# Another hand-written order for the first batch of a fused attention and MLP kernel, with four copies moved between engines

## The chip, the cores and the metric

The kernel runs on one core of a Trainium2 chip. The core has five engines with instruction queues of their own, each worked off strictly in order: TensorE (PE, matrix products and transposes), VectorE (DVE), ScalarE (ACT), GpSimd (POOL) and SyncE (SP, which only issues transfers here). They wait for each other through semaphores. The metric is the device time of one execution in microseconds, the median of several runs.

## The reference

Eight batches of 448 tokens, 12 heads of 64. Queries and keys are normalised per head, attention follows, and its output goes, as 768 channels per token, through a layer norm and a two-layer MLP with a residual:

```
q_n, k_n = rmsnorm(q, g_q), rmsnorm(k, g_k)
attn     = softmax(q_n @ k_n^T / sqrt(64))
x        = (attn @ v) as [batch, 448, 768]
xn       = layernorm(x) * g_ln
out      = x + relu(xn @ w_ch1) @ w_ch2        # 768 -> 3072 -> 768
```

All inputs and the output are float32; the kernel multiplies in float16 with float32 sums.

## The kernel before

**Stages.** Attention of batch 0 runs first and alone. From then on attention of batch b+1 is woven between the matrix products of the MLP of batch b; a planner (`attention`, `run_rest`) does that by costs. Only the first stage is ordered by hand: `ORDER` (L39) is a list of words, which `first_attention` (L502) reads from left to right, recording one piece of work for each. Each engine's queue is the subsequence of these pieces that it takes part in. So moving a word moves an instruction in its engine's queue only, and past the others only as far as semaphores say.

**Tiles.** Two heads make a pair; batch 0 has pairs 0 to 5. Pairs come in units: unit 0 is pair 0, unit 1 is pair 1, unit 2 is pairs 2 and 3, unit 3 pairs 4 and 5; units 4 to 6 belong to batch 1 and are prepared towards the end of the stage. A pair's 448 x 2 tokens lie as seven groups of 128 rows, so a unit has 448 elements per partition for each pair (7 groups of 64).

**Words that prepare a unit u** (`pieces`, L237):
- `a`, `c`: squares of keys and queries (L261 on POOL for what `POOL_SQUARE` lists, L263 on ACT otherwise)
- `d`, `e`: their sums (L269, DVE); `gq`, `gk`, `g`: reciprocal root, two ACT steps (L272, L273)
- `i`: keys times the gain product (L283; on DVE for units in `DVE_KG`, on POOL otherwise); for unit 0 it also makes the gain product, through PE
- `j`: the keys' float16 high part (L289 on POOL for `POOL_HI`, L291 on ACT otherwise); `k`: the low part, a subtraction (L294; POOL for `POOL_LO`, DVE otherwise)
- `l`: scaled queries (L86, DVE); `m`: a second copy of them next to the first, so that one transpose fills both halves of the partitions (L334 on ACT for `ACT_DUP`, L336 on POOL for `POOL_DUP`, on DVE otherwise; nothing for units in `TWICE`)
- `z`: values to float16 (L341, L347, POOL)

**Words that work on a pair p:**
- `Kp`: seven transposes of the keys (high and low part side by side, L377 and L380) into one bank `tr`, copied to `kU` (L383 on ACT for `ACT_K`, L385 on DVE otherwise)
- `Qp`: seven transposes of the queries (L397; in a unit of `TWICE` each group is transposed twice, into the upper and the lower 64 partitions), copied to `qU` (L400 on ACT for `ACT_Q`, L402 on DVE otherwise)
- `Sp.i`: scores of group i (L417; for i = 6 two products, L427 and L428) and their exponential on ACT (L433), called Ep.i below. Two score banks alternate, so a score waits for the exponential two before it; nine tiles E alternate, so an exponential also waits for an older `V`.
- `Vp.i`: probabilities times values (L470, L472); after i = 6 DVE divides by the sums (L485 to L492) and so frees the banks for the pair after next
- `Hn`, `Jn`: n filler products of PE whose results nobody reads (L544, L547)

**Other words.** `T` statistics of finished pairs (L653), `A` their aggregate (L668), `Nt` and `Xt` layer norm (L674) and transposes (L710, copied on ACT for t = 0 and 1, on DVE at L718 for t = 2), `R` its root, `Ut` the first up-projections, six products for each of three columns of blocks (L956); `W` loads of MLP weights, `G`, `G2` the layer norm's gain (load and scaling), `L` loads of a unit, `M` some minima. What follows the list begins with the up-projections at L730.

The pieces that the change moves to another engine are these lines:

```
DVE_KG, POOL_HI, POOL_DUP, ACT_Q = (0, 6), (1, 2, 3, 4, 5, 6, *range(8, 25)), (3, 4, 5, 6), (0, 2, 4, 5)
ACT_K, ACT_DUP = (), ()
TWICE = ()
POOL_SQUARE, POOL_LO = ((2, 1), (4, 0), (6, 0), (7, 0), (7, 1)), (5, 6)
```

Of the kernel before, what the change touches and what calls it, by code (L numbers as in the profile page):

```python
# [24 lines left out]
PAIR_UNIT = [(u, w) for u, (_, _, m) in enumerate(UNITS) for w in range(m)]  # L25
UNIT_PAIR = [PAIR_UNIT.index((u, 0)) for u in range(len(UNITS))]
EXP_BIAS = -4.0
DVE_KG, POOL_HI, POOL_DUP, ACT_Q = (0, 6), (1, 2, 3, 4, 5, 6, *range(8, 25)), (3, 4, 5, 6), (0, 2, 4, 5)
ACT_K, ACT_DUP = (), ()
END_WORK = 44  # L30
TWICE = ()
POOL_SQUARE, POOL_LO = ((2, 1), (4, 0), (6, 0), (7, 0), (7, 1)), (5, 6)

# [1 line left out]


ORDER = """  # L39
b0 H12 a0 L4 c0 i0 e0 j0 H24 b1 gq0 d0 k0 l0 a1 m0 K0 G gk0 i1 H10 L5 c1 Q0 d1 j1 H8 S0.0 b2  # L40
S0.1 H5 a2 e1 g1 S0.2 c2 S0.3 k1 l1 z0 d2 e2 m1 K1 S0.4 i2 H16 S0.5 S0.6 H12 Q1 g2 H5 J8 b3 l2
j2 k2 c3 V0.0 S1.0 z2 S1.1 S1.2 V1.0 J8 a3 m2 H4 V0.1 z3 S1.3 K2 S1.4 V0.2 Q2 V0.3 V0.4 d3 S1.5
V0.5 V0.6 S2.0 S1.6 V1.1 V1.2 S2.1 e3 W0 i3 K3 V2.0 S2.2 V2.1 S2.3 Q3 j3 T0 S2.4 k3 V1.3 g3 V1.4
S2.5 S2.6 l3 b4 V1.5 m3 c4 S3.0 S3.1 V2.2 S3.2 K4 a4 V1.6 S3.3 V2.3 S3.4 Q4 d4 V2.4 V2.5 V3.0
V3.1 V3.2 V2.6 i4 S3.5 j4 J4 S3.6 V3.3 T1 K5 e4 k4 S4.0 W1 S4.1 S4.2 Q5 z4 b5 S4.3 V3.4 V4.0
V3.5 S4.4 V4.1 V4.2 S4.5 W2 V4.3 S5.0 g4 V3.6 S4.6 S5.1 J4 V5.0 V4.4 G2 S5.2 l4 T3 K6 V4.5 V5.1
V4.6 S5.3 T4 V5.2 a5 L6 V5.3 S5.4 m4 Q6 i5 S5.5 V5.4 S5.6 V5.5 V5.6 T5 S6.0 S6.1 J4 S6.2 A V6.0
S6.3 V6.1 N0 N1 S6.4 S6.5 J4 V6.2 X0 V6.3 d5 j5 N2 S6.6 V6.4 X1 z5 Q7 c5 V6.5 R U0 e5 U1 g5 X2
V6.6 M k5 U2 K7 b6 L7 a6 L8k c6 i6 l5 m5 e6
""".split()  # L50
DMA_UNIT = 7
PE_SET = (DMA_UNIT + 1) % 2
# [42 lines left out]
class _Fast:  # L95
# [141 lines left out]
    def pieces(self, u):  # L237
# [91 lines left out]
        def qdup():  # L329
            if u in TWICE:  # L330
                return
            out, x = c["qn"][:, :, 1], c["qn"][:, :, 0]
            if u in ACT_DUP:
                nc.scalar.copy(out=out, in_=x)  # L334
            else:
                (nc.gpsimd if u in POOL_DUP else nc.vector).tensor_copy(out=out, in_=x)  # L336
# [50 lines left out]
    def trans_q(self, p):  # L387
# [6 lines left out]
        for i in (6, *range(6)):  # L394
            o, g = ps[:, :, 384:S] if i == 6 else ps[:, i // 3, ts(i % 3, 128)], self.group(p, i)
            for r in (slice(0, D), slice(D, 2 * D)) if u in TWICE else (slice(0, 2 * D),):
                nc.tensor.matmul(o[r], qn[:, g, 0] if u in TWICE else qn[:, g], sh.id16,  # L397
                                 is_transpose=True, start=(i == 6), stop=(i == 5))
# [866 lines left out]
```

## Time and profile before

| | |
|---|---|
| median of 3 runs | 578.69 us (578.44 to 578.82) |
| the profiled execution | 578.23 us, its span 576.7 us |
| PE busy | 563.6 us, 98% of the span |
| DVE busy | 385.5 us, 67% |
| ACT busy | 363.4 us, 63% |
| POOL busy | 210.0 us, 36% |

The span runs from the first to the last instruction on the chip; some 1.5 us of the time lie outside it. The trace lists every instruction with start, duration, engine, line of the code and tile. In a row of the timeline the columns are start, duration (us), engine, line, operation, output and inputs with their shapes, how many alike were merged, and in brackets the idle time before it with what ended it. An engine's next instruction can start somewhat before the end shown of the one before, since ends overlap in a pipeline. A table of windows gives, for each stretch of the span, each engine's busy time and number of instructions.

### The profile page before, as it was taken

To read this page: it belongs to the slowest core of one execution; us is meant where nothing else is said; L and a number is where in the kernel's file an instruction comes from. 1 tells how busy PE (TensorE), PEld (TensorE's weight loads), DVE (VectorE), ACT (ScalarE), POOL (GpSimd) and SP (SyncE) were. 2 spreads that over 40 slices of the span, in tenths; PEclk is the share of its full clock that TensorE was granted. 3 is DMA by queue.
4 is the path that set the end of the run, shared out by engine and by line. 5 is a ranking of instruction groups with operands and counts; after the bars stand their busy time and mean duration, and the time that the engine had idled before them with its cause. 6 is when DMAs were issued, how large, how long until landed. Compare 5 with 4: busy or idle time off the path is not lost.

```text
span 576.7 us, 13800 instructions
## 1 busy us (share of the span) xinstructions
PE 563.6 (98%) x5510; PEld 416.5 (72%) x5510; DVE 385.5 (67%) x832; ACT 363.4 (63%) x672; POOL 210.0 (36%) x226
## 2 busy tenths in 40 slices
PE   6888999999999999999999999999999999999999
PEld 5656666687686867777677768777777777878686
DVE  6989578799757586846667586854756743664424
ACT  5998886457674779457675588647777477323130
POOL 4885855404540721554341521654242410020000
PEclk9999999999999999999999999999999999999999
DMA  8999999968573877968563787958753390030302
GB/s 215 272 237 221 212 200 165 170 180 111 124 134 84 145 151 141 127 140 116 124 91 66 183 139 143 117 139 141 129 62 65 120 112 2 1 109 1 84 2 59
DMA packets 175321, 72.59 MB, mean 126 GB/s; under 512 B 138292, under 2 KB 170212, under 8 KB 175252
## 3 DMA queue, kind: packets, MB, share of 16 engines
q1 hardware_dynamic: 134304, 52.75, 43.9%
q0 software_dynamic: 40352, 18.50, 24.1%
q8 instruction: 44, 0.72, 0.5%
q10 hardware_dynamic: 596, 0.41, 0.3%
q14 instruction: 25, 0.20, 0.1%
HBM read 52.76 MB, written 11.01 MB: 111 GB/s over the span
## 4 chain that ended last, share of the span: by engine, by line
PE 92%; DVE 3%; ACT 3%; issue 1%; DMA 0%; ACTq 0%; DVEq 0%
PE psH L809 34%; PE psP L832 30%; PE psS L417 8%; PE oA L470 5%; PE psC L740 4%; PE psH L730 4%; ACT E L433 2%; PE oB L472 2%; PE psS L423 2%; DVE ssq L269 1%; PE psW L544 1%; PE tr L380 1%; ACT qU L400 0%; PE psW L1003 0%; DMA w<-in_g_k_dram 0%
## 5 line engine op out<-in xcount | busy, mean ns | idle before, releaser
L433 ACT ACTIVATE E<-psS,rr_all 128x448 f16<-128x448 f32 x336 | 204.1, 633 | 49.1 <-PE psS L417 40.4
L809 PE MATMUL psH<-xnT,w 128*128 128x256 f16 (+1 forms) x2016 | 225.7, 261 | 0.0
L809 PEld LDWEIGHTS <-w 128*128 128x128 f16 x2016 | 172.8, 98 | 24.4 <-issue 5.0
L812 ACT ACTIVATE hS<-psH 128x512 f16<-128x512 f32 x150 | 89.7, 598 | 98.0 <-PE psH L809 93.3
L832 PEld LDWEIGHTS <-hS 128*128 128x128 f16 x1080 | 100.0, 98 | 57.4 <-issue 1.1
L832 PE MATMUL psP<-w,hS 128*128 128x384 f16 x672 | 127.0, 326 | 0.0
L417 PE MATMUL psS<-qU,kU 128*128 128x448 f16 x288 | 101.0, 352 | 4.4 <-ACT E L433 2.9
L470 PEld LDWEIGHTS <-E 128*128 128x128 f16 x1008 | 70.3, 98 | 35.6 <-issue 2.6
L283 POOL TENSOR_TENSOR k<-k,gprod 128x896 f32<-128x896 f32 x18 | 39.2, 2180 | 139.8 <-ACT khl L263 86.1
L815 DVE TENSOR_TENSOR hS<-hS 128x512 f16<-128x512 f16 (+1 forms) x119 | 58.3, 496 | 19.3 <-ACT hS L812 17.8
L832 PE MATMUL psP<-w2s,hS 128*128 128x384 f16 (+1 forms) x408 | 69.9, 322 | 0.0
L470 PE MATMUL oA<-v,E 128*128 128x65 f16 x864 | 66.8, 194 | 1.1 <-ACT E L433 0.6
L768 DVE SCALAR_TENSOR_TENSOR x<-psP,rs_all,x 128x384 f32<-128x384 f32 x60 | 36.4, 616 | 41.1 <-PE psP L832 40.5
L472 PE MATMUL oB<-v,E 128*128 128x65 f16 x288 | 52.0, 193 | 0.1
L843 POOL TENSOR_TENSOR x<-x,hS 128x384 f32<-128x384 f32 x21 | 23.4, 1126 | 75.3 <-ACT hS L911 74.6
L485 DVE RECIPROCAL rec_all<-oA 128x6 f32<-128x6 f32 x48 | 9.2, 192 | 53.0 <-PE oA L470 52.9
L220 POOL DMA_DIRECT2D v<-in_v_dram x54 | 41.5, 781 | 4.4 <-PE oB L472 3.3
L417 PEld LDWEIGHTS <-kU 128*128 128x128 f16 x288 | 28.1, 98 | 10.7 <-issue 2.0
L911 ACT ACTIVATE hS<-hS,rs_all 128x384 f32<-128x384 f32 x27 | 14.6, 604 | 33.0 <-DVE hS L815 33.0
L472 PEld LDWEIGHTS <-E 128*128 128x128 f16 x336 | 32.4, 97 | 0.3 <-DVE xl L492 0.2
L86 DVE SCALAR_TENSOR_TENSOR qn<-q,rr_all 128x256 f16<-128x256 f32 (+2 forms) x69 | 25.0, 424 | 6.8 <-ACT rr_all L273 6.7
L269 DVE TENSOR_REDUCE ssq<-khl 128x14 f32<-128x896 f32 (+1 forms) x24 | 25.5, 1061 | 3.7 <-ACT khl L263 3.6
(145 smaller groups left out, 630.5 us busy)
## 6 DMA issues: line engine op xcount, KB each, us to landing
k<-in_k_dram SPq DMA_DIRECT2D x19, 384.0 KB, 4.3
q<-in_q_dram SPq DMA_DIRECT2D x18, 384.0 KB, 4.1
out_dram<-x SPq DMA_DIRECT2D x14, 384.0 KB, 3.0
w<-in_moe_w_ch_dram POOLq DMA_DIRECT2D x3, 1536.0 KB, 14.5
w<-in_moe_w_ch_dram POOLq DMA_DIRECT2D x4, 1152.0 KB, 14.1
v<-in_v_dram POOLq DMA_DIRECT2D x54, 64.0 KB, 4.4
out_dram<-x POOLq DMA_DIRECT2D x9, 384.0 KB, 2.7
qU<-qn SPq DMA_TRANSPOSE x90, 2.9
```

Source lines behind the costliest of these rows:

```text
L220: nc.gpsimd.dma_start(out[:, :, j, 0:D], main[:, :, j])
L269: nc.vector.tensor_reduce(out=c["ssq"][:, n], in_=c["sq", n], axis=AX.X, op=ALU.add)
L283: (nc.vector if u in DVE_KG else nc.gpsimd).tensor_tensor(out=c["t"][1], in0=c["t"][1], in1=sh.gprod.unsqueeze(1).broadcast_to([128, g, D] ...
L417: nc.tensor.matmul(ps[0][:, 0:S], c["main"][:, ts(i, 128)], c["q"][:, ts(h, S)], start=True, stop=True)
L433: nc.scalar.activation(out=o, in_=x[:, 0:S], func=AFT.Exp, scale=self.units[u][3][:, g:g + 1], bias=EXP_BIAS)
L470: nc.tensor.matmul(oA[:, t, cs], E[:, ts(t, 128)], rhs, start=(i == 0 and t == 0), stop=(i == 6 and t == 2))
L472: nc.tensor.matmul(oB[:, cs], E[:, 320:448], rhs, start=(i == 0), stop=(i == 6))
L768: self.nc.vector.scalar_tensor_tensor(out=x, in0=ps, scalar=self.rs[:, b, t:t + 1], in1=x, op0=ALU.mult, op1=ALU.add)
L809: nc.tensor.matmul(ps[:, i], sh.w1[:, dc, ts(f + i, 128)], self.xnT[:, dc, 256 - N:256], start=(i == 0 and dc == 0), stop=(i == k - 1 and ...
L812: nc.scalar.activation(out=hT[:, f:f + k], in_=ps, func=AFT.Relu)
L815: nc.vector.tensor_tensor(out=out, in0=a, in1=c, op=op)
L832: nc.tensor.matmul(bank[x][:, c], a[:, f], w[:, f, c], start=(start and f == 0), stop=(stop and f == HALF - 1))
```

## The change

It gives some pieces of the first stage another engine:

- unit 1's queries are not doubled (`m1` does nothing) but transposed twice on PE (`TWICE`): fourteen transposes of 64 columns instead of seven of 128
- pair 1's keys are copied out of `tr` by ACT instead of DVE
- the queries of pairs 0, 2 and 5 are copied by DVE instead of ACT (pair 4's stay on ACT)
- unit 0's doubling goes from DVE to ACT
- unit 1's high part goes from POOL to ACT
- unit 2's product with the gains goes from POOL to DVE
- unit 4's low part goes from DVE to POOL, unit 6's from POOL to DVE; unit 6's square of queries from POOL to ACT

And it writes the order anew. Of the words moved, these meet the longest queues: unit 0's `c` and `j` go ahead of the 24 fillers, ten fillers go from before `Q0` to behind it, `a1` goes behind `m0`, the sum `d3` goes ahead of the copies of `K2` and `Q2`, the first weight load `W0` behind `j3` on POOL, `l4` ahead of `T3` and `K6`, the scaling of the layer norm's gain (`G2`) behind `m4`, `X2` ahead of `U1`, `K7` and `l5` ahead of `U2`. Fillers are 121 instead of 128. The order of the loads on SP stays as it was.

```diff
-DVE_KG, POOL_HI, POOL_DUP, ACT_Q = (0, 6), (1, 2, 3, 4, 5, 6, *range(8, 25)), (3, 4, 5, 6), (0, 2, 4, 5)
-ACT_K, ACT_DUP = (), ()
+DVE_KG, POOL_HI, POOL_DUP, ACT_Q = (0, 2, 6), (2, 3, 4, 5, 6, *range(8, 25)), (3, 4, 5, 6), (4,)
+ACT_K, ACT_DUP = (1,), (0, 1)
 END_WORK = 44
-TWICE = ()
-POOL_SQUARE, POOL_LO = ((2, 1), (4, 0), (6, 0), (7, 0), (7, 1)), (5, 6)
+TWICE = (1,)
+POOL_SQUARE, POOL_LO = ((2, 1), (4, 0), (7, 0), (7, 1)), (4, 5)
 
 ORDER = """
-b0 H12 a0 L4 c0 i0 e0 j0 H24 b1 gq0 d0 k0 l0 a1 m0 K0 G gk0 i1 H10 L5 c1 Q0 d1 j1 H8 S0.0 b2
-S0.1 H5 a2 e1 g1 S0.2 c2 S0.3 k1 l1 z0 d2 e2 m1 K1 S0.4 i2 H16 S0.5 S0.6 H12 Q1 g2 H5 J8 b3 l2
-j2 k2 c3 V0.0 S1.0 z2 S1.1 S1.2 V1.0 J8 a3 m2 H4 V0.1 z3 S1.3 K2 S1.4 V0.2 Q2 V0.3 V0.4 d3 S1.5
-V0.5 V0.6 S2.0 S1.6 V1.1 V1.2 S2.1 e3 W0 i3 K3 V2.0 S2.2 V2.1 S2.3 Q3 j3 T0 S2.4 k3 V1.3 g3 V1.4
-S2.5 S2.6 l3 b4 V1.5 m3 c4 S3.0 S3.1 V2.2 S3.2 K4 a4 V1.6 S3.3 V2.3 S3.4 Q4 d4 V2.4 V2.5 V3.0
-V3.1 V3.2 V2.6 i4 S3.5 j4 J4 S3.6 V3.3 T1 K5 e4 k4 S4.0 W1 S4.1 S4.2 Q5 z4 b5 S4.3 V3.4 V4.0
-V3.5 S4.4 V4.1 V4.2 S4.5 W2 V4.3 S5.0 g4 V3.6 S4.6 S5.1 J4 V5.0 V4.4 G2 S5.2 l4 T3 K6 V4.5 V5.1
-V4.6 S5.3 T4 V5.2 a5 L6 V5.3 S5.4 m4 Q6 i5 S5.5 V5.4 S5.6 V5.5 V5.6 T5 S6.0 S6.1 J4 S6.2 A V6.0
-S6.3 V6.1 N0 N1 S6.4 S6.5 J4 V6.2 X0 V6.3 d5 j5 N2 S6.6 V6.4 X1 z5 Q7 c5 V6.5 R U0 e5 U1 g5 X2
-V6.6 M k5 U2 K7 b6 L7 a6 L8k c6 i6 l5 m5 e6
+b0 a0 b1 L4 H18 i0 c0 j0 H24 e0 k0 gq0 l0 G d0 m0 a1 gk0 K0 Q0 H10 c1 d1 L5 S0.0 i1 e1 g1 j1 S0.1
+b2 l1 H14 c2 k1 S0.2 a2 H4 d2 e2 i2 m1 z0 j2 S0.3 K1 S0.4 S0.5 Q1 H8 g2 b3 S0.6 c3 J11 S1.0
+S1.1 H20 V0.0 k2 a3 l2 z2 H3 V0.1 m2 S1.2 S1.3 H7 d3 K2 i3 z3 Q2 V0.2 S1.4 V0.3 e3 V0.4 V1.0
+V1.1 V0.5 S1.5 j3 V1.2 V0.6 S2.0 T0 S2.1 S1.6 W0 K3 S2.2 k3 V1.3 S2.3 S2.4 g3 Q3 V2.0 V2.1 S2.5
+S2.6 V2.2 l3 V1.4 S3.0 b4 V1.5 S3.1 V1.6 m3 S3.2 K4 V2.3 a4 S3.3 c4 V3.0 S3.4 V3.1 i4 V2.4 Q4 d4
+V2.5 S3.5 e4 V2.6 S3.6 j4 K5 S4.0 Q5 W1 S4.1 S4.2 b5 V4.0 S4.3 V3.2 k4 z4 V3.3 V3.4 S4.4 V3.5 T1
+V4.1 V4.2 W2 S5.0 g4 V3.6 S4.5 l4 S4.6 S5.1 J1 S5.2 m4 V4.3 V5.0 S5.3 T3 K6 S5.4 V4.4 V5.1 V5.2
+V4.5 V4.6 L6 a5 T4 S5.5 V5.3 V5.4 Q6 S5.6 G2 V5.5 V5.6 T5 S6.0 A S6.1 V6.0 S6.2 S6.3 V6.1 J1
+S6.4 N0 V6.2 N1 S6.5 i5 d5 j5 V6.3 X0 S6.6 V6.4 N2 X1 z5 V6.5 Q7 c5 e5 g5 U0 X2 U1 R V6.6 K7 l5
+U2 M k5 m5 L7 L8k b6 a6 i6 c6 e6
```

## The prediction

> **What bounds the kernel now.** PE is busy nearly throughout, so I read first the busy time by stage (each column an engine).
>
> ```profile
> core 0: us, PE busy (x) PEld busy (x) DVE busy (x) ACT busy (x) POOL busy (x), PEclk, DMA share, GB/s
> 0.00:12.53 12.53, 7.74 (x71) 7.03 (x72) 7.63 (x21) 5.84 (x12) 4.92 (x12) 1.00 0.83 204
> 12.53:56.44 43.91, 36.81 (x497) 26.72 (x497) 40.94 (x80) 39.24 (x76) 32.74 (x32) 1.00 1.10 245
> 56.44:576.70 520.26, 519.02 (x4947) 382.74 (x4944) 336.90 (x734) 318.30 (x586) 172.36 (x184) 1.00 0.65 114
> ```
> From 56.44 us on (first up-projection matmul of batch 0 outside U) PE is idle for 520.26 - 519.02 = 1.2 us in all. The change leaves that part's PE work alone, so it is worth what it moves the moment at which that part begins. Before it lie two stages: up to the first score at 12.53, and 43.9 us in which DVE is busy 93% and ACT 89%.
>
> The timelines of ACT and DVE there say which of the two waits for which.
>
> ```profile
> 11.57 0.91 ACT L400 COPY qU<-psQ 128x896 f16<-128x896 f16 x1 [1.81 <-PE psQ L397]
> 12.91 1.16 ACT L433 ACTIVATE E<-psS,rr_all 128x448 f16<-128x448 f32 x2 [0.44 <-PE psS L417]
> 23.72 0.92 ACT L400 COPY qU<-psQ 128x896 f16<-128x896 f16 x1
> 24.51 1.20 ACT L433 ACTIVATE E<-psS,rr_all 128x448 f16<-128x448 f32 x2
> 29.03 2.76 ACT L433 ACTIVATE E<-psS,rr_all 128x448 f16<-128x448 f32 x5
> 37.29 0.90 ACT L400 COPY qU<-psQ 128x896 f16<-128x896 f16 x1
> 42.70 0.63 ACT L433 ACTIVATE E<-psS,rr_all 128x448 f16<-128x448 f32 x1 [0.41 <-PE psS L417]
> 44.07 2.02 ACT L433 ACTIVATE E<-psS,rr_all 128x448 f16<-128x448 f32 x3
> ```
> E0.0 starts at 12.91. An exponential takes 0.63 and the next follows after (2.76 - 0.63)/4 = 0.53. E2.0, the second of the pair at 24.51, starts at 24.51 + 1.20 - 0.63 = 25.08. E5.6, the last of the three at 44.07, starts at 44.07 + 2.02 - 0.63 = 45.46. From 24.51 on only one gap of ACT (0.41) shows: there ACT sets the pace. A query copy (Q2's at 23.72, Q5's at 37.29) holds it 24.51 - 23.72 = 0.79.
>
> ```profile
> 9.52 1.11 DVE L336 COPY qn<-qn 128x448 f16<-128x448 f16 x1
> 10.55 0.64 DVE L385 COPY kU<-tr 128x960 f16<-128x960 f16 x1
> 12.44 2.08 DVE L294 TENSOR_TENSOR khl<-w2s,khl 128x448 f16<-128x448 f32 x1 [0.20 <-POOL khl L289]
> 16.61 1.07 DVE L269 TENSOR_REDUCE ssq<-qn 128x14 f32<-128x896 f32 x1
> 19.16 0.62 DVE L402 COPY qU<-psQ 128x896 f16<-128x896 f16 x1
> 22.08 0.48 DVE L336 COPY qn<-qn 128x896 f16<-128x896 f16 x1
> 38.59 1.08 DVE L294 TENSOR_TENSOR khl<-k,khl 128x896 f16<-128x896 f32 x1
> 48.48 0.49 DVE L668 BATCH_NORM_AGGREGATE stat<-stat 128x2 f32<-128x24 f32 x3
> 54.43 0.56 DVE L718 COPY w2s<-tr 128x768 f16<-128x768 f16 x1
> 57.76 1.79 DVE L283 TENSOR_TENSOR k<-k,gprod 128x896 f32<-128x896 f32 x1
> ```
> ```profile
> 8.93 1.55 POOL L283 TENSOR_TENSOR w2s<-w2s,gprod 128x448 f32<-128x448 f32 x1 [4.92 <-ACT khl L263]
> 12.37 1.68 POOL L261 TENSOR_TENSOR khl<-w2s 128x896 f32<-128x896 f32 x1
> 16.28 2.08 POOL L283 TENSOR_TENSOR w2s<-w2s,gprod 128x896 f32<-128x896 f32 x1
> 18.42 0.93 POOL L289 CAST khl<-w2s 128x896 f16<-128x896 f32 x1
> 19.29 0.83 POOL L341 CAST v<-w 128x768 f16<-128x768 f32 x1
> 55.07 1.89 POOL L294 TENSOR_TENSOR khl<-hS,khl 128x896 f16<-128x896 f32 x1
> 56.92 1.68 POOL L261 TENSOR_TENSOR qn<-q 128x896 f32<-128x896 f32 x1
> ```
> These two belong together. The copy at 9.52 takes 1.11 for half the elements of the one at 22.08 (0.48), and ends 0.15 after POOL's product (8.93 + 1.55). The subtraction at 12.44 takes 2.08 for half the elements of the one at 38.59 (1.08), beside POOL's square (to 14.05). So DVE's two-operand operations and SBUF copies stand still until POOL's running one ends; reductions and copies out of PSUM do not. The Trainium skill, "SBUF — State Buffer", section "Who interferes with whom", calls it an exclusive lock on a shared port pair, where the second to issue blocks fully; the 0.15 us agrees. By it, the key product that the change gives to DVE costs 1.08 or 1.79 by POOL's work beside it.
>
> **The change part by part.** I follow each engine's queue in the new order, with these durations; 0.05 us stands for a signal between engines, an estimate from PE's 12.53 behind the copy's end at 12.48.
>
> ```profile
> 6.32 2.74 PE L544 MATMUL psW<-id 128*128 128x128 f16 x24
> 9.09 0.85 PE L380 MATMUL tr<-id,khl 128*128 128x128 f16 x6
> 10.80 0.74 PE L397 MATMUL psQ<-id,qn 128*128 128x128 f16 x7
> 12.53 0.54 PE L417 MATMUL psS<-qU,kU 128*128 128x448 f16 x2 [0.55 <-ACT qU L400]
> 17.26 0.83 PE L544 MATMUL psW<-id 128*128 128x128 f16 x12
> 19.85 0.55 PE L417 MATMUL psS<-qU,kU 128*128 128x448 f16 x2
> 55.04 1.17 PE L956 MATMUL psU<-w2s,w 128*128 128x128 f16 x18 [0.42 <-DVE w2s L718]
> ```
> *Start.* Unit 0's duplication (L334, 448 elements) goes to ACT: 0.58, as ACT's squares of that size (row below); bounds 0.58 and the 0.91 of the 896-element copy; I take 0.58. The query scaling, which now ends where the copy at 9.52 starts, has one sum less ahead of it and ends at about 9.2; ACT's duplication then at 9.8. K0 still ends at 9.94 (9.09 + 0.85). Q0 follows at once, without ten fillers between, at PE's slow rate of the start (2.74/24 = 0.11 each): to 10.75. DVE, no longer in the blocked copy, takes it in 0.62: 11.4. S0.0 starts at 11.45 and E0.0 at 11.83 (12.91 - 12.53 = 0.38 later), 1.08 before now.
>
> ```profile
> 9.18 0.58 ACT L263 ACTIVATE qn<-w2s 128x448 f32<-128x448 f32 x1
> 13.96 0.22 ACT L272 ACTIVATE rt<-ssq 128x14 f32<-128x14 f32 x1
> 14.21 0.22 ACT L273 ACTIVATE rr_all<-rt 128x14 f32<-128x14 f32 x1
> ```
> *Pairs 0 and 1.* Unit 1's key square is now behind the duplication on ACT, so POOL's product starts at 10.35 instead of 8.93 and ends at 11.4, the square of unit 2 at 13.1. DVE's two sums of unit 1 (half of 1.07 each) end at 12.45, the root (two steps, 0.25 each) at 12.96. The scaling waits for POOL's square: 13.6. POOL's value cast slips in (0.83), the subtraction ends at 14.85. Two sums (1.0 apart) bring 16.85, the key product of unit 2 on DVE 17.85. I take 1.08 for it, since POOL has nothing to do until it is finished; the other bound is 1.79. Q1's 14 half transposes run 16.2 to 17.0 (0.056 each; (0.83 - 0.2)/11 from the fillers at 17.26); even at 0.11 each they end by 17.8, so TWICE costs nothing and spares DVE a copy and POOL's port a turn. K1's copy on ACT, 0.91 to 0.98 by size, ends at 16.8, a microsecond ahead of need. Q1's copy ends at 18.45: S1.0 at 18.5 instead of 19.85, 1.35 earlier.
>
> *Pair 2.* POOL's high part (0.93, now behind DVE's product) ends at 18.85 and its value cast follows before DVE's subtraction can start: blocked to 19.6. Subtraction 20.55, scaling 21.65, duplication 22.15, the sum of unit 3 placed ahead 23.15, copies of K2 and Q2 (both DVE) 23.7 and 24.25. E2.0 starts at 24.7, only 0.4 before now: DVE, with Q2's 0.6 and the product's 1.0 added, gives back most of the lead. Bounds: 23.9 if the subtraction is not blocked, 25.3 if one more POOL cast gets in.
>
> *Pairs 2 to 5.* E2.0 to E5.6 take 45.46 - 25.08 = 20.38 now. Q5's copy leaves ACT (0.79) and costs DVE 0.62, which in turn loses unit 4's subtraction to POOL (1.08 for 1.89; needed by K6 at about 41, ready at 38). That is 19.6. Of the rest 28 x 0.53, Q4's copy and two squares (0.79 each by that copy, of their size) and two roots (0.4 each) make 18.0, so up to 1.6 are waits for scores; the new order of PE, followed score by score, has about 0.8 of them less. I take half, 19.2: E5.6 at 43.9, 1.6 earlier. Bounds of this stage: 18.8 and 20.4.
>
> *To the multiplication layers.* DVE's chain from E5.6's end to the aggregate (48.48) and to X2's copy (54.43) holds the same instructions. X2 stands before U1 and K7 before U2; both wait for the same two DVE copies, and U2 with K7 are the same PE work in either order. The shift passes whole: 1.6.
>
> *Hidden.* Fillers: 128 become 121, 0.056 each; the ten before S0.0 end with the copy that it waits for, the twenty before V0.0 run while ACT holds unit 3's square. First weight load: it moves behind POOL's high part of unit 3, to some 26.6; by the row below it lands at about 41, well ahead of U0 to U2 (U2 at 55.04). Unit 6: its query square goes from POOL (1.68) to ACT (0.9), its subtraction from POOL to DVE; both lie after U2, ahead of work that PE needs some 1 us later at the earliest. Without that cover they cost 0.9 and 1.1.
>
> ```profile
> w<-in_moe_w_ch_dram POOLq DMA_DIRECT2D x3, 1536.0 KB, 14.5
> ```
>
> Sum: 578.23 (profiled execution) - 1.6 = 576.6. The median stands 0.46 above that execution, so 577.1.
>
> **Rivals.** *The lead is lost at the port.* If POOL's key product of unit 3 (2.08) starts before DVE's duplication of unit 2, that duplication waits some 1.8 us, E2.0 comes at 26.5, 1.4 late; Q5's 0.8 and half a microsecond of fewer waits come off: 578.8. For it: the blocked copy at 9.52. Against: scaling stands directly ahead of the duplication and POOL has still a cast to run, so only that fits between. With scores waiting as now throughout (E2.0 to E5.6 19.6) and E2.0 at 25.0 the gain is 0.85: 577.8. Together 0.24.
>
> *PE's clock falls back (slower).* Between H14's end (12.6) and K1 (14.9) PE has four fillers and one score; if that idling brings the slow rate of 6.32 back for as long as at the start (6.32 to Q0's end at 11.5), the work from S0.4 to S1.0 (14 half transposes, 19 fillers, four score matmuls: 2.6 us at the fast rate) takes 2.6 more, then twenty fillers 1.1 more, of which ACT's square of unit 3 hides 0.9. It decides from S0.4 on: 2.8 - 1.6 = 1.2 slower, 579.9. For it: only five matmuls stand in those 2.3 us. Against: the longest gap is 1.1 us. The Trainium skill, "TensorE: Matmul & The Clock Gate", section "Why this matters for your kernels", asks for gaps over about 3 us; by that it stays fast, and no run here shows where it falls. With other late waits of that size: 0.16.
>
> *More is gained.* Subtraction unblocked (E2.0 at 23.9) and all fewer waits: 0.8 + 0.4 more, 575.9: 0.10.
>
> **How the numbers follow.** Forecast 577.1 with 0.50 (its own range 576.4 to 577.7), port 0.24, clock and late waits 0.16, more 0.10. 0.2% (1.16 us, about what a measurement tells from no change) lies at 577.53 and 579.85. Faster: 0.10 + 0.42 of the forecast + 0.06 of the port case = 0.58. Slower: most of the clock case and a tail of port, 0.15. The rest, 0.27, is no change. The range runs from 575.8 to 579.3: above it most of the clock case, below it a tail of the best.
>
> **What would show it.** Right: E0.0 near 11.8, S1.0 near 18.5, E2.0 near 24.7, E5.6 near 43.9, aggregate near 46.9, X2's copy ending near 53.4; DVE's key product of unit 2 at 1.08. Wrong: the duplication of unit 2 far above 0.48; fillers at 0.11 after 12 us; a PE gap behind U2; E2.0 after 25.1.

## The result: slower in the median, though the first 55 us went as walked

| | before | after |
|---|---|---|
| median | 578.37 us (9 runs) | 581.36 us (9 runs) |
| lowest to highest | 577.88 to 578.82 | 576.88 to 583.89 |
| profiled execution | 578.23, span 576.7 | 576.88, span 575.3 |

The ratio is 1.0045, with a 95% interval of 1.0027 to 1.0063; a second series of the same kernel gave 1.0022 (1.0000 to 1.0043). The prediction of 577.1 (575.8 to 579.3) was wrong, and so was its direction. The executions of the kernel before agree within 1 us, those of the changed one scatter over 7 us, and the profiled one happens to be the lowest of its nine. So its trace shows where the first stage gained, but not what cost the others.

Busy time by stage, after, split at the first score's exponential and at the first up-projection matmul outside U:

```profile
core 0: us, PE busy (x) PEld busy (x) DVE busy (x) ACT busy (x) POOL busy (x), PEclk, DMA share, GB/s
0.00:11.70 11.70, 8.12 (x69) 7.47 (x70) 6.53 (x19) 5.41 (x12) 4.10 (x11) 1.00 0.81 203
11.70:54.68 42.98, 36.57 (x500) 26.25 (x498) 39.99 (x79) 38.24 (x75) 33.41 (x32) 1.00 1.08 241
54.68:575.30 520.62, 519.31 (x4945) 382.87 (x4943) 337.58 (x737) 319.00 (x587) 168.82 (x182) 1.00 0.66 115
```

The up-projections begin at 54.68 instead of 56.44, and what follows takes as long as before (520.6, with 1.3 us of PE idle). The timelines of ACT, DVE, POOL and PE, after:

```profile
12.07 0.63 ACT L433 ACTIVATE E<-psS,rr_all 128x448 f16<-128x448 f32 x1 [1.05 <-PE psS L417]
...
23.94 4.33 ACT L433 ACTIVATE E<-psS,rr_all 128x448 f16<-128x448 f32 x7 [0.16 <-PE psS L417]
...
42.72 1.23 ACT L433 ACTIVATE E<-psS,rr_all 128x448 f16<-128x448 f32 x2
...
56.63 0.95 ACT L263 ACTIVATE qn<-q 128x896 f32<-128x896 f32 x1 [0.40 <-DMA q<-in_q_dram]
```
```profile
16.79 1.08 DVE L283 TENSOR_TENSOR w2s<-w2s,gprod 128x896 f32<-128x896 f32 x1
...
18.97 1.68 DVE L294 TENSOR_TENSOR khl<-w2s,khl 128x896 f16<-128x896 f32 x1 [0.56 <-POOL khl L289]
21.78 0.39 DVE L336 COPY qn<-qn 128x896 f16<-128x896 f16 x1
...
46.51 0.49 DVE L668 BATCH_NORM_AGGREGATE stat<-stat 128x2 f32<-128x24 f32 x3
...
52.53 0.55 DVE L718 COPY w2s<-tr 128x768 f16<-128x768 f16 x1
```
```profile
18.88 0.83 POOL L341 CAST v<-w 128x768 f16<-128x768 f32 x1
```
```profile
16.27 0.58 PE L397 MATMUL psQ<-id,qn 128*64 128x128 f16 x14
...
18.46 0.68 PE L417 MATMUL psS<-qU,kU 128*128 128x448 f16 x2
18.98 1.28 PE L544 MATMUL psW<-id 128*128 128x128 f16 x20
```

| step | predicted | trace of after |
|---|---|---|
| E0.0 starts | 11.8 | 12.07 |
| key product of unit 2 on DVE | 1.08 | 1.08 |
| S1.0 starts | 18.5 | 18.46 |
| unit 2's subtraction ends, held by POOL's cast | 20.55 | 18.97 + 1.68 = 20.65 |
| E2.0 starts (second of the seven at 23.94; by itself in the trace) | 24.7 | 24.7 |
| E5.6 starts (second of two at 42.72: 42.72 + 1.23 - 0.63) | 43.9 | 43.3 |
| aggregate | 46.9 | 46.51 |
| X2's copy ends | 53.4 | 53.08 |

One row of ACT was not in the plan: at 56.63 unit 6's query square waits 0.40 for its load. The transfers' view (queue, count, size, us from issue to landing) has the reason. First before, then after:

```profile
q<-in_q_dram SPq DMA_DIRECT2D x1, 384.0 KB, 6.4
```
```profile
q<-in_q_dram SPq DMA_DIRECT2D x1, 384.0 KB, 20.7
```

Before, the load was issued at 35.3 and landed at 41.7. After, it was issued at 32.7 and landed at 53.4, and its left-over rows (two transfers of 32 KB), issued until some 37, came 19 to 21 us later. Even this lowest execution only just made it.

### The profile page after: what moved, and what is told of

It reads as the page before. It is cut to its first block, busy times and chain, and to the rows that moved or that the text cites. A ratio compares the mean times of both kernels' runs of the same rounds, so it can differ in the third digit from the quotient of the medians.

```text
span 575.3 us, 13792 instructions
## 1 busy us (share of the span) xinstructions
PE 564.0 (98%) x5510; PEld 416.6 (72%) x5510; DVE 384.1 (67%) x833; ACT 362.6 (63%) x673; POOL 206.3 (36%) x223
## 4 chain that ended last, share of the span: by engine, by line
PE 90%; DMA 8%; SPq 2%; ACT 0%; issue 0%; ACTq 0%
PE psH L809 35%; PE psP L832 30%; PE psS L417 8%; PE oA L470 5%; PE psC L740 4%; DMA q<-in_q_dram 3%; PE psH L730 3%; DMA hS<-in_v_dram 2%; PE psS L423 2%; PE oB L472 2%; DMA k<-in_k_dram 1%; SPq L157 1%; DMA w<-in_v_dram 1%; SPq L149 1%; DMA w2s<-in_q_dram 1%; PE psW L1003 0%
## 5 line engine op out<-in xcount | busy, mean ns | idle before, releaser
L832 PEld LDWEIGHTS <-hS 128*128 128x128 f16 x1080 | 100.0, 98 | 57.4 <-issue 1.1
```

The costliest lines, as they stand in the source:

```text
L832: nc.tensor.matmul(bank[x][:, c], a[:, f], w[:, f, c], start=(start and f == 0), stop=(stop and f == HALF - 1))
```

## The experiments

Seventeen runs, in five series. Each series has its own runs of the kernel before (medians 578.41, 578.49, 578.46, 578.30, 578.42; highest executions 579.1, 580.0, 580.2, 579.6, 579.7). The changed kernel itself was repeated in the first series only, so the later ones are read against the kernel before and against each other.

| label | change | landing of the query load in the profile, us | executions, us | median | ratio, 95% |
|---|---|---|---|---|---|
| e1_again | after, unchanged | 17.4 | 576.7 to 583.2 | 579.24 | 1.0022 (1.0000 to 1.0043) |
| e2_fill_early | after, more fillers at 13 to 17 us | 20.7 (left-over rows) | 576.5 to 583.7 | 580.41 | 1.0035 (1.0014 to 1.0057) |
| e3_fill_late | after, more fillers at 36 to 47 us | 24.8 | 576.6 to 583.2 | 579.89 | 1.0026 (1.0003 to 1.0050) |
| e4_before_no16 | before, 16 fillers fewer | 12.2 | 578.1 to 579.3 | 578.61 | 1.0002 (0.9993 to 1.0011) |
| f1_square_pool | after, unit 6's square on POOL | 21.3 | 577.9 to 581.0 | 578.67 | 1.0008 (0.9996 to 1.0019) |
| f2_w0_early | after, first weights early | 19.1 | 576.9 to 583.7 | 580.17 | 1.0029 (1.0010 to 1.0048) |
| f3_before_act | before, unit 6's square on ACT | 12.1 | 577.9 to 578.7 | 578.32 | 0.9999 (0.9990 to 1.0008) |
| f4_c6_late | after, the square some steps later on ACT | 23.9 | 576.9 to 582.4 | 580.40 | 1.0028 (1.0012 to 1.0044) |
| g1_w1_w2_late | after, second and third weights late | 7.0 | 575.4 to 580.3 | 577.08 | 0.9983 (0.9966 to 1.0001) |
| g2_w1_behind_k4 | after, second weights 1.1 us later | 8.4 | 576.4 to 582.7 | 577.15 | 0.9985 (0.9967 to 1.0004) |
| g3_before_w1_early | before, square on ACT, second weights early | 21.2 | 578.4 to 581.2 | 579.17 | 1.0014 (1.0003 to 1.0025) |
| h1_w0_early_rest_late | g1 and first weights early | 7.9 | 576.5 to 584.3 | 579.09 | 1.0027 (1.0002 to 1.0051) |
| h2_all_late | g1 and second layer's weights late | 9.8 | 576.1 to 577.6 | 576.38 | 0.9971 (0.9962 to 0.9980) |
| h3_before_late | before, second and third weights late | 6.1 | 577.7 to 579.3 | 578.46 | 1.0003 (0.9995 to 1.0012) |
| i1_w0_early_all_late | h2 and first weights early | 14.1 | 577.2 to 583.6 | 578.32 | 1.0012 (0.9991 to 1.0032) |
| i2_second_layer_late | after, second layer's weights late | 20.1 | 576.6 to 583.7 | 581.07 | 1.0037 (1.0015 to 1.0059) |
| i3_h1_again | h1, unchanged | 12.9 | 577.1 to 583.6 | 580.36 | 1.0023 (1.0001 to 1.0045) |

The landing is that of the one profiled execution, which need not be typical of its kernel.

### First series: is it the clock?

I began with the prediction's slower rival and took the scatter for PE's clock: two versions put fillers where the change had thinned PE's work, one took fillers from the kernel before.

```diff
 e2_fill_early
-S0.2 a2 H4 d2 e2 i2 m1 z0 j2 S0.3 K1 S0.4 S0.5
+S0.2 a2 H18 d2 e2 i2 m1 z0 j2 S0.3 H9 K1 S0.4 H4 S0.5
 e3_fill_late
-V2.6 S3.6 ... S5.1 J1 S5.2 ... S6.1 V6.0 S6.2 S6.3 V6.1 J1
+V2.6 J4 S3.6 ... S5.1 J4 S5.2 ... S6.1 J4 V6.0 S6.2 S6.3 V6.1 J4
 e4_before_no16 (from the kernel before)
-i2 H16 S0.5
+i2 S0.5
```

> The changed kernel unchanged, to see an execution of the common kind (8 of the 9 timed so far lie 3 to 7 us above the profiled one, 576.88). Theory A (the matmul clock falls back in the thin stretch between H14 and H8, 13.0 to 16.8 us): times scatter again, 579 to 584, and a profile of a slow execution shows fillers and 128-column transposes at about 0.11 us each instead of 0.056 from some point between 13 and 21 us. Theory B (it falls back later, between 36 and 47 us, where J fillers were taken out): the same times, but slow matmuls only after 36 us. Theory C (no clock, but late transfers): all matmuls at 0.056 after 12 us and idle PE behind a DMA.

> The changed kernel with 27 more fillers in the thin stretch: 18 instead of 4 behind S0.2, 9 behind S0.3, 4 behind S0.4, all in time in which PE waited in the profiled execution. Theory A: every execution at 576.5 to 577.5, like the profiled one of the changed kernel. Theories B and C: scatter stays, 579 to 584.

> The changed kernel with fillers back in the later stretch: four more ahead of S3.6, three more behind S5.1, four behind S6.1, three more behind V6.1. Theory B: executions at 576.5 to 577.5. Theories A and C: scatter stays, 579 to 584.

> The kernel before without the sixteen fillers behind S0.4 (15.2 to 16.1 us). Theory A: its thin stretch then runs from 12 to 17 us, so executions scatter as those of the changed kernel do, 579 to 585 beside 578.4 of the kernel before. Theories B and C: no scatter, 578.4 within 0.5.

The repetition scatters again, both versions with fillers scatter as much, and the kernel before doesn't scatter without its sixteen. Both clock theories fall. But the profiled execution of the late fillers was a long one, with a span of 581.5, and it shows the place. ACT and PE in it:

```profile
54.70 0.96 ACT L263 ACTIVATE khl<-k 128x896 f32<-128x896 f32 x1
60.22 0.95 ACT L263 ACTIVATE qn<-q 128x896 f32<-128x896 f32 x1 [4.55 <-DMA q<-in_q_dram]
61.08 0.85 ACT L733 ACTIVATE hS<-psH 128x384 f16<-128x384 f32 x2
```
```profile
56.74 0.65 PE L730 MATMUL psH<-w2s,w 128*128 128x384 f16 x3
61.60 1.12 PE L730 MATMUL psH<-w2s,w 128*128 128x384 f16 x3 [4.21 <-ACT hS L733]
...
64.97 1.94 PE L730 MATMUL psH<-w2s,w 128*128 128x384 f16 x6
...
68.00 1.14 PE L730 MATMUL psH<-w2s,w 128*128 128x384 f16 x6
```

ACT's queue is strict. Unit 6's query square, given to ACT by the change, stands at its head and waits 4.55 us for the load. Behind it stand the relu copies (L733) that free the banks of the up-projections, so PE stops for 4.21 us. Then six matmuls take 1.94 instead of 1.14. The windows of that execution give the granted clock (the column of 0.98, 0.50, 0.84):

```profile
55.00:60.00 5.00, 2.39 (x15) 1.30 (x14) 2.74 (x9) 0.67 (x1) 2.61 (x3) 0.98 1.11 241
60.00:65.00 5.00, 3.40 (x16) 1.91 (x16) 2.08 (x2) 4.16 (x8) 1.51 (x2) 0.50 1.16 222
65.00:70.00 5.00, 5.00 (x32) 2.87 (x31) 3.28 (x4) 3.00 (x9) 0.72 (x3) 0.84 1.15 225
```

Half speed from the gap's end to some 66.7 costs about 2.5 us more. Gap and slow clock are 4.2 + 2.5 = 6.7 us together, and this span is 581.5 - 575.3 = 6.2 us longer than the one profiled for the changed kernel. The clock does fall, then, but as a consequence. The Trainium skill, "TensorE: Matmul & The Clock Gate", section "Why this matters for your kernels", asks for no gap over some 3 us between matmuls; the 4.21 us here agree.

The wait also goes with the time from trace to trace. In six profiled executions that keep the square at this place and the second and third weights where the change put them, ACT waits for this load 0 us (execution of 576.54, e2_fill_early), 0.40 (576.88, the changed kernel), 0.66 (576.66, e1_again), 1.97 (578.58, i2_second_layer_late), 3.65 (583.70, f2_w0_early) and 4.55 (583.07, e3_fill_late). And a slow clock isn't needed for a long execution: of the changed kernel's nine, the one of 580.37 had a mean granted clock of 1.000, as the lowest had.

### Second series: the square's engine and place, the first weights' place

```diff
 f1_square_pool
-POOL_SQUARE, POOL_LO = ((2, 1), (4, 0), (7, 0), (7, 1)), (4, 5)
+POOL_SQUARE, POOL_LO = ((2, 1), (4, 0), (6, 0), (7, 0), (7, 1)), (4, 5)
 f2_w0_early
-d3 K2 i3 z3 ... S1.6 W0 K3
+d3 K2 W0 i3 z3 ... S1.6 K3
 f3_before_act (from the kernel before)
-POOL_SQUARE, POOL_LO = ((2, 1), (4, 0), (6, 0), (7, 0), (7, 1)), (5, 6)
+POOL_SQUARE, POOL_LO = ((2, 1), (4, 0), (7, 0), (7, 1)), (5, 6)
 f4_c6_late
-b6 a6 i6 c6 e6
+b6 a6 i6
```

> The changed kernel, with unit 6's query square back on POOL. Theory D (what costs is that this square stands in ACT's queue ahead of the relu copies of the first up-projections and waits there for unit 6's query load, which lands 17 to 25 us after its issue; PE then stands still for some 4 us and runs slowly for some 5 us after): the scatter of 0 to 7 us between executions goes, the median falls from 581.4 (first series) and 579.2 (second) to about 577.0 (576.5 to 577.6), ratio to the kernel before 0.997 to 0.998. On POOL the late load holds up only POOL's and DVE's preparation of unit 6. Rival E (the crowded transfer engines delay something else too, the weights or the other loads of units 5 and 6, whatever engine takes the square): the scatter stays, median 578.5 to 580.

> The changed kernel, with only the first weight load moved on POOL from behind the high part of unit 3 to ahead of its product with the gains (where it was before the change). Theory D with its second half (the query load lands late because the three weight loads of 1.5 MB now follow 9 and 5 us apart instead of 12.5 and 2, and the first is still on its way when the query load is issued): landing time of unit 6's query load falls from 20 us to 6 to 14 us, ACT's square waits for nothing, no scatter, median 577.0 (576.4 to 577.8). If the place of the weight load is not what makes it late: landing stays at 17 to 25 us, scatter of 0 to 7 us stays, median 579 to 581.

> The kernel before, with unit 6's query square on ACT instead of POOL and nothing else. If the square on ACT needs the late load to do harm (theory D in both halves): the load lands at about 46 to 51 us, well ahead of the square at some 56, the ratio is 1.000 (0.998 to 1.002) and no execution is over 580. If ACT's 0.95 us ahead of the relu copies costs by itself: ratio 1.0015, without scatter. If this square on ACT is enough to do harm in any order: scatter up to 584, ratio 1.002 to 1.005.

> The changed kernel, with unit 6's query square and its sum taken out of the hand-written list, so that the planner puts them some steps later, among the up-projections: the square stays on ACT and the load stays late. Theory D (it is the place in ACT's queue ahead of the first relu copies that hurts): most of the scatter goes, median 576.8 to 577.8. Rival E (the crowded transfers hurt elsewhere): scatter stays, median 579 to 581. If the planner's place is still too early for executions whose load lands latest (at some 60 us): a smaller scatter, up to 2 us.

The square on ACT does no harm by itself: in the kernel before it gives 0.9999. With the square back on POOL the highest executions are gone, but the median falls only to 578.67, not to 577: the late load now holds up another queue. Rows of its waits (who, on whom, us in all, times, longest) and of its PE:

```profile
DVE ssq L269 <- POOL qn L261: 3.1, 1, 3.1
```
```profile
63.45 0.90 PE L397 MATMUL tr<-id,qn 128*128 128x128 f16 x7 [2.65 <-DVE kU L385]
```

DVE's sum waits for POOL's square, the copy of unit 6's keys stands behind that sum, and PE needs the bank that this copy frees. Moved some steps later on ACT, the square leaves the first relu copies free and then holds up an exponential. ACT and PE of that kernel:

```profile
59.84 0.95 ACT L263 ACTIVATE qn<-q 128x896 f32<-128x896 f32 x1 [2.62 <-DMA q<-in_q_dram]
```
```profile
61.36 0.35 PE L417 MATMUL psS<-qU,kU 128*128 128x448 f16 x1 [2.39 <-ACT E L433]
```

So my theory had the wrong half in front. At each of the three places tried, something that PE needs stands behind the square; the cause is the late load. The first weight load alone, put back, doesn't make it early: it landed 19.1 us after its issue, with ACT waiting 3.65 us.

### Third series: the pause between two weight loads

The view of the transfer queues (packets, MB, share of the 16 engines) shows what the loads meet. Software_dynamic is POOL's queue, which carries the weights, hardware_dynamic SP's. The kernel before, 30 to 35 us, with the first weight load on its way:

```profile
q0 software_dynamic: 422, 0.86, 91.7%
q1 hardware_dynamic: 416, 0.19, 20.5%
```

As many packets from each, but 2.0 KB against 0.46 KB. By these counts the two queues take turns packet by packet, so as long as weights are on their way SP's loads move 0.19 / 5 = 0.04 MB a microsecond, against 0.26 in the pause that follows (1.03 / 4, below). The Trainium skill, "DMA: Bandwidth & Descriptors", section "Queues, rings and completion order", says that each engine goes round its queues by the packet; 422 against 416 agrees. Then the pause until the second weight load, before (36 to 40 us) and after (38 to 40 us):

```profile
q1 hardware_dynamic: 1786, 1.03, 94.6%
q0 software_dynamic: 77, 0.14, 18.2%
```
```profile
q1 hardware_dynamic: 1052, 0.59, 101.5%
q0 software_dynamic: 28, 0.04, 10.5%
```

Before, 1.03 MB come through in the pause, unit 6's queries among them. After, only 0.59 MB: the first weight load was issued 2.65 us later (26.42 for 23.77) and ends later, and the second 0.8 us earlier (35.44 for 36.27). What hasn't come through by then waits beside 3 MB of weights. After, 40 to 45 us:

```profile
q0 software_dynamic: 399, 0.82, 86.0%
q1 hardware_dynamic: 470, 0.28, 25.4%
```

```diff
 g1_w1_w2_late
-Q5 W1 S4.1 ... V4.2 W2 S5.0 ... S5.6 G2 V5.5
+Q5 S4.1 ... V4.2 W1 S5.0 ... S5.6 G2 W2 V5.5
 g2_w1_behind_k4
-Q5 W1 S4.1 ... k4 z4
+Q5 S4.1 ... k4 W1 z4
 g3_before_w1_early (from f3_before_act)
-V2.6 i4 ... S4.0 W1 S4.1
+V2.6 W1 i4 ... S4.0 S4.1
```

> The changed kernel, with the second weight load moved to where the third stood (POOL at some 40 instead of 35.4) and the third behind the scaling of the layer norm's gain (some 44). Theory G (while a weight load is on its way, SP's queue gets one small packet for each 2 KB packet of the weights and moves 0.15 to 0.3 MB in 5 us instead of 1.0 to 1.2; unit 6's query load lands early only if it gets through in the pause between the end of the first weight load, at 38, and the first packets of the second, some 4 us after its issue, at 40 in the changed kernel): the pause grows from 2 us to some 6, SP moves over 1 MB between 38 and 44, unit 6's query load lands by 46, nothing waits for it, no scatter: median 577.0 (576.4 to 577.6), ratio 0.997 to 0.998, no execution over 578.5. If the place of the second weight load is not it: the load lands at 53 to 60 and the executions scatter up to 583 as before, median 579 to 581. If the weights now come late instead: PE waits in the up-projections on the second block of weights at some 60 us, over 1 us, in every execution.

> The changed kernel, with only the second weight load moved, behind unit 4's low part on POOL: 1.9 us later (37.3 instead of 35.4), the third where it was. Theory G: the pause is 3.5 to 4 us instead of 2, as long as in the kernel before (36.3 to 39.8); the query load gets through in most executions: median 577.0 to 578, a small scatter left at most (up to 581 in one or two of twelve). If the pause has nothing to do with it: as the changed kernel, median 579 to 581, up to 583.

> The kernel before with unit 6's query square on ACT (which alone cost nothing) and the second weight load 3 us earlier on POOL, ahead of unit 4's product with the gains (33.2 instead of 36.3). Theory G: the second load's packets follow the first's without a pause; unit 6's query load lands at 53 to 60 and ACT waits for it ahead of the first relu copies: scatter as in the changed kernel but around the kernel before, 578 to 585, median 580 to 583. If it needs the changed order of the rest: no scatter, median 578.3.

The first two went the expected way in the median, but the first was to have no execution over 578.5, and three of its twelve stand at 579.6 to 580.3. With the second and third weight loads later, SP moved 1.03 MB between 37 and 41:

```profile
q1 hardware_dynamic: 1864, 1.03, 96.3%
q0 software_dynamic: 69, 0.12, 15.8%
```

The query load lands 7.0 us after its issue and the median is 577.08. One microsecond for the second load alone (its issue at 36.50 in the trace, not the 37.3 expected) already brings 577.15, with two executions of twelve at 579.2 and 582.7. The intervals of both ratios just pass 1. In the kernel before, an earlier second weight load, with the square on ACT, makes the load as late as after (21.2 us) and raises the median to 579.17 (ratio 1.0014, 1.0003 to 1.0025), less than the 580 to 583 that I wrote; its highest execution, 581.2, is little above the 580.2 of the kernel before in that series, so this run shows the late load clearly and its scatter hardly. It landed at 36.3 + 21.2 = 57.5, just ahead of the square at 58.0, which stands 1.4 us later there.

How much got through in the pause also tells traces with the second weights unmoved apart. Between 37 and 40 us SP moved 0.60 to 0.62 MB in the three that came out lowest (the changed kernel, e1_again, e2_fill_early), 0.43 in f4_c6_late and 0.39 in e3_fill_late, where ACT waited 2.62 and 4.55 us. It isn't the whole rule: i2_second_layer_late moved 0.65 and waited 1.97.

### Fourth and fifth series: the scatter that was left

Of the three high executions with later second and third weights none was profiled. Either the pause was still too short, or the next loads, unit 7's, met the next weights: after has the second layer's first weights at 57.4 instead of 61.6.

```diff
 h1_w0_early_rest_late (from g1)
-d3 K2 i3 z3 ... S1.6 W0 K3
+d3 K2 W0 i3 z3 ... S1.6 K3
 h2_all_late (from g1)
-W2_AT = 47, 71
+W2_AT = 51, 71
 h3_before_late (from the kernel before)
-S4.0 W1 S4.1 ... S4.5 W2 V4.3 ... V4.4 G2 S5.2
+S4.0 S4.1 ... S4.5 W1 V4.3 ... V4.4 G2 W2 S5.2
```

> The changed kernel with all three weight loads moved: the first back ahead of unit 3's product with the gains (POOL at some 21), the second where the third stood (some 38 to 40), the third behind the scaling of the layer norm's gain (some 42 to 44). Theory G: the first load ends at some 34, so the pause until the second's packets grows from 3 us (second and third late only) to 6 or more, and unit 6's query load gets through in every execution: no execution over 578.5, median 576.0 to 576.8. If what scatter was left with the second and third late has another cause (the loads of unit 7, the clock): the same share of executions at 579 to 580.5, median 577.

> The changed kernel with the second and third weight loads late as before, and the first load of the second layer's weights four of the planner's steps later as well, behind unit 6's high part on POOL (61 instead of 56, where the kernel before has it). Rival for the scatter that was left (three of twelve executions at 579.6 to 580.3): it is unit 7's loads, held up by these weights, since in the changed kernel weights follow each other from 40 to 76 without a pause. Then: no execution over 578.5, median 576 to 576.8. If what is left comes from unit 6's query load still: about three of twelve at 579.5 to 580.5, median 577.

> The kernel before with its second and third weight loads late in the same way (the second where the third stood, the third behind the scaling of the gain). Theory G: there the query load already got through in the pause and nobody waited for it, so nothing is gained: ratio 1.000 (0.998 to 1.001), median 578.4, without scatter. If the later weights gain something by themselves: ratio below 0.998, and the gain of the changed kernel with late weights is not that of the change.

With the second layer's weights late as well no scatter is seen: eleven executions between 576.05 and 577.62, ratio 0.9971. The kernel before gains nothing from later weights (1.0003); the second layer's stand in both at the same time (issued at 61.57 here, 61.55 in the kernel before). With the first weights early the scatter came back in full, against the expectation. The last three runs ask why, and whether the second layer's weights alone would have been enough.

```diff
 i1_w0_early_all_late (from h1)
-W2_AT = 47, 71
+W2_AT = 51, 71
 i2_second_layer_late (from after)
-W2_AT = 47, 71
+W2_AT = 51, 71
 i3_h1_again: h1, unchanged
```

> The kernel with the first weight load early and the second and third late (which scattered from 576.5 to 584.3), and the first load of the second layer's weights four planner's steps later as well. If its scatter came from these weights, which hold up the loads of units 7 and 8 (theory G carried on to the next loads): gone, median 576.4 (576.0 to 577.0), no execution over 578. If the early first weight load does the harm, by slowing the loads of units 4 to 6 from 23 us on: it stays, median 578 to 580.

> The changed kernel with nothing else than the first load of the second layer's weights four planner's steps later (61 instead of 57). If unit 6's query load is the cause in the changed kernel, these weights, issued at 57 when it has landed or nearly so, can hardly help it: scatter as in the changed kernel, median 579 to 581, up to 583. If most of the scatter came from units 7 and 8: median 576.5 to 577.5.

> The same kernel as with the first weight load early and the second and third late, once more, for its profile of another execution: if one above 578.5 is caught, its trace shows either ACT waiting for unit 6's query load near 56 (the pause did not suffice) or, with that one landed, PE waiting some 2 to 6 us for work on unit 7 or 8 after 65 whose load came late. Times as before: median 577.5 to 580, up to 584.

The repetition caught a long execution (span 580.3), and in it unit 6 is nearly in time (a wait of 0.21) while unit 7 is late. POOL, PE and the windows of that execution:

```profile
72.41 1.67 POOL L261 TENSOR_TENSOR khl<-w2s 128x896 f32<-128x896 f32 x1 [5.53 <-DMA w2s<-in_k_dram]
74.16 2.07 POOL L283 TENSOR_TENSOR w2s<-w2s,gprod 128x896 f32<-128x896 f32 x1
78.65 1.68 POOL L261 TENSOR_TENSOR qn<-w2s 128x896 f32<-128x896 f32 x1 [2.41 <-DMA w2s<-in_q_dram]
```
```profile
76.15 0.25 PE L470 MATMUL oA<-v,E 128*128 128x65 f16 x3 [2.10 <-DVE x L487]
...
82.53 0.35 PE L417 MATMUL psS<-qU,kU 128*128 128x448 f16 x1 [2.29 <-ACT E L433]
```
```profile
70.00:75.00 5.00, 4.05 (x31) 2.27 (x30) 1.14 (x2) 3.46 (x7) 2.51 (x2) 1.00 1.15 224
75.00:80.00 5.00, 3.77 (x40) 2.59 (x40) 1.50 (x6) 1.96 (x3) 2.59 (x2) 1.00 0.85 196
80.00:85.00 5.00, 2.21 (x24) 1.40 (x23) 4.61 (x9) 2.83 (x8) 3.77 (x6) 1.00 1.12 204
```

POOL waits 5.53 us for unit 7's keys and 2.41 for its queries, and PE is idle for 15 - 10.03 = 5.0 us between 70 and 85. The other profiled execution of the same kernel (h1_w0_early_rest_late, span 575.0) has no such waits and is 580.3 - 575.0 = 5.3 us shorter. Again strict queues pass the wait on: DVE's sums stand still until POOL's squares are done (3.86 us before the one at 74.12, 3.73 before the one at 80.36), and the divisions and, through the root on ACT, the exponentials that PE waits for stand behind them. In the version without scatter the same square starts at 67.53 and waits for no load:

```profile
67.53 1.67 POOL L261 TENSOR_TENSOR khl<-w2s 128x896 f32<-128x896 f32 x1 [0.42 <-PE tr L380]
```

With all later weights late and only the first early, scatter stays (577.2 to 583.6), and its profile has unit 6 late again, by 2.18 us of ACT. Early first weights run beside the loads of units 4 to 6: SP moved 0.84 + 0.47 = 1.31 MB there between 20 and 30 us, 1.17 + 0.75 = 1.92 in the kernel before, and the query load was issued at 39.9 instead of 35.3. So a longer pause after an earlier start won nothing here; I take it that what counts is how much SP's queue has moved by the time the second weights begin, but no run sets that amount alone. Late second-layer weights alone leave the changed kernel as it was (581.07). So unit 6's load is the main cause. That unit 7's made the three high executions left in g1_w1_w2_late is argued from i3_h1_again, whose first weights come early; the intervals of g1 and h2 overlap (0.9966 to 1.0001 and 0.9962 to 0.9980), and g1's lowest execution, 575.41, is below h2's 576.05.

The version with the second, third and fourth weight loads late is faster than the kernel before: 576.38 against 578.30, ratio 0.9971 (0.9962 to 0.9980).

## Why the prediction was wrong

- *The first stage* was right. All steps up to X2's copy came within 0.6 us, and the shift at the first up-projection outside U is 56.44 - 54.68 = 1.8 us where I summed 1.6. Two smaller errors partly cancel in it: E2.0 to E5.6 took 43.3 - 24.7 = 18.6, under my lower bound of 18.8 where I took 19.2, which makes E5.6 2.1 earlier; and of that shift, which was to pass whole, 0.4 was lost by the up-projection. With the loads in time the whole change is worth 578.30 - 576.38 = 1.9 us. My forecast of 577.1 is 0.7 above that version and 4.3 below the changed kernel.
- *TWICE, the fillers, DVE's and POOL's turns at the port* were right: the fourteen half transposes took 0.58 at 16.27, twenty fillers 1.28 at 18.98 (0.056 each and not 0.11), the key product 1.08, the duplication 0.39, and the subtraction was held as walked (1.68). The port rival did not happen.
- *The clock rival* had the wrong place and the wrong cause: fillers in the thin stretch change nothing. Its price, a slow clock for some microseconds, does appear, but after a gap that a late load made. Its chance of 0.16 also held "other late waits of that size" and named none.
- *The step that failed* is the one called "Hidden", in two sentences. "Unit 6: its query square goes from POOL (1.68) to ACT (0.9)" was to lie "ahead of work that PE needs some 1 us later at the earliest", and "without that cover" to cost 0.9. That prices the instruction and not its wait. I took the load for landed because nothing waited for it before; its landing stands nowhere in the prediction. The price was 4.2 us of PE gap and about 2.5 us of half clock in the long execution that was profiled (e3_fill_late; both profiled executions of the changed kernel itself are among its lowest). The same step undid the last term of the sum, the 0.46 by which the median stands above the profiled execution: after the change that distance is 581.36 - 576.88 = 4.5. The profiled execution itself, 576.88, is close to the 576.6 that was summed for it.
- That the first weight load lands "well ahead of U0 to U2" held, and was the wrong question. I asked who waits for the weights, not which loads stand beside them. That the second load also moved, 0.8 us earlier and ahead of unit 4's low part, I didn't price at all, and the list of moved words above doesn't have it; nor the second layer's load, 4 us earlier because POOL's queue is shorter. (That list also names `c0`, `j0` and `l4`: they stood ahead of the 24 fillers, of `T3` and of `K6` already.)
- The prediction's own check, "a PE gap behind U2", was the right place to look. It isn't in the profile of after, because that execution was the lowest.

Shown are the late loads, the waits for them in several profiled executions, and that later weights take the scatter away with the rest of the change kept. Not shown is why, with the same kernel, the load comes just in time in one execution and, as the times suggest, some microseconds too late in the next.

## What to carry to other kernels

When an edit moves a step that reads a fresh load, price the step's wait by the load's latest landing, and list what stands behind it on that engine: a strict queue turns one late load into a stall of whatever comes next. Bulk weight loads on another queue are not free when nobody waits for them; place them by what small loads must pass in the pauses between them. And where a median and a profile disagree, take profiles of more executions before believing either: here the one trace at hand showed every gain and none of the cost.

## What the runs showed of the hardware that was not expected

- The same 384 KB load takes 6.4 us from issue to landing when it gets into a pause of the weights, and 17 to 25 us when most of it doesn't (6.4, 17.4, 20.7, 24.8 in four traces). Between them lie 12.1 and 12.2 in f3_before_act and e4_before_no16, which have the order of before but issue it 3 us later, and 12.9 and 14.1 in i3_h1_again and i1_w0_early_all_late. One microsecond in the start of the second weight load went with 8.4 instead of 20.7 (g2_w1_behind_k4).
- PE gaps of 1.64 us (i1_w0_early_all_late) and 2.39 us (f4_c6_late) left the granted clock at 1.00, one of 2.65 us (f1_square_pool) was followed by 0.82 and 0.84 in the next two windows of 5 us, and one of 4.21 us (e3_fill_late) by 0.50. So in this one execution a gap somewhat under the 3 us that the Trainium skill names ("TensorE: Matmul & The Clock Gate", "Why this matters for your kernels") cost clock already.
